# Local attention and a top-128 feed-forward on one core: 570 listed steps in place of nested loops

## The chip, the cores and the metric

The kernel runs on one core of a Trainium2 chip. The metric is device time in microseconds for one execution, median of several. The engines are PE (TensorE, with its weight loads shown as PEld), DVE (VectorE), ACT (ScalarE), POOL (GpSimd) and SP (SyncE, which here only issues DMAs). Each engine works through its own instructions in order; semaphores join them.

## The reference

q, k and v are 4 batches x 8 heads x 768 positions x 64 in float32. Attention is local: 24 chunks of 32 queries, each against 8 memory rows, 16 positions to the left, its own 32 and 8 to the right. The result x (4 x 768 x 512) goes through a gated feed-forward that touches only 128 rows of each batch:

```python
a = np.exp(scores - np.max(scores, axis=-1, keepdims=True))
out[:, :, c_start:c_end] = np.matmul(a / (a.sum(-1, keepdims=True) + 1e-09), v_full)
# then, for each batch b of x
scores = x @ w_gate
top_idx = np.argpartition(-scores[b], capacity)[:capacity]
h = np.maximum(x[b, top_idx] @ w1, 0.0)
ye = h @ w2
out[b, top_idx] = x[b, top_idx] + sigmoid(scores[b, top_idx])[:, None] * ye
```

w1 is 512 x 1024 and w2 is 1024 x 512.

## The kernel before, in words

Two heads make a pair, four pairs a batch: 16 pairs, n = 0 to 15. Each load brings 96 partitions of 8 positions for several heads, cast to 16 bit on the way, from POOL's DMA queue (`load`, L76); k, q and v come in groups of 2 or 4 heads, the memory rows and pads in four early DMAs and three from SP, the weights in two DMAs (`load_w`, L406).

A pair is worked in these parts. `t_k`, `t_q`, `t_v`: 16 PE transposes each into one PSUM bank (L161), an ACT copy out (L169, L172), and for k and v a small POOL copy that repeats the memory rows in every segment (L179, L185). `v_win`: 24 window transposes and 24 small products with the gate weights, alternating (L196, L197), then two DVE copies and one on ACT (L200, L202). `scores`: 48 products (L212) and a DVE maximum (L218). `soft`: four products that subtract the maximum (L226) and the exponential on ACT (L230). `t_p`: 12 transposes (L240) and a DVE copy, tile PT (L243). `values`: 48 products with 66 columns, of which column 64 is the sum of the probabilities and 65 the gate score (L260); DVE divides (L267 to L273), POOL casts the pair's columns of x to 16 bit for the gather (L275).

When a batch's four pairs are through, twelve expert steps go into a queue (`moe_steps`, L386): store x, spread the gate scores along rows, six compares on DVE (L318), counts on PE (L326), a scan over the mask (L334) and the slots, a one-hot selection, a gather by 24 products (L348), index and gate sums (L357), two halves of the first FFN product (L371), the second (L380), and a scatter that adds to the stored rows (L383). The main loop takes up to three of these steps in each round, between the parts of pairs n + 1 and n + 2; after the last pair the rest run one behind the other.

The order is that of the program text. Banks: one pair of banks for the scores, one for the values, four that turn for everything else.

Of the kernel before, what the change touches and what calls it, by code (L numbers as in the profile page):

```python
# [26 lines left out]
def kernel(  # L27
# [28 lines left out]
    VW = 66  # L56

    ctx.enter_context(tc.manual_schedule())

# [430 lines left out]
```

## Time and profile before

| | us |
|---|---|
| median of 3 runs (lowest, highest) | 192.08 (191.09, 194.02) |
| the profiled execution, its own time | 189.55 |
| its span in the trace | 187.8 |
| PE, DVE, ACT, POOL busy | 125.4, 92.9, 64.0, 55.0 |

The span runs from the first to the last instruction that the profiler recorded. Matmuls are pipelined, so their durations overlap; the distance between the starts of two groups is the better measure. Where an engine stood before an instruction, the trace names what ended the standing; "issue" means that nothing it shows did. DMA share is the mean busy share of 16 DMA engines and passes 1 where transfers overlap.

### The profile page before, as it was taken

To read this page: it belongs to the slowest core of one execution; us is meant where nothing else is said; L and a number is where in the kernel's file an instruction comes from. 1 tells how busy PE (TensorE), PEld (TensorE's weight loads), DVE (VectorE), ACT (ScalarE), POOL (GpSimd) and SP (SyncE) were. 2 spreads that over 40 slices of the span, in tenths; PEclk is the share of its full clock that TensorE was granted. 3 is DMA by queue.
4 is the path that set the end of the run, shared out by engine and by line. 5 is a ranking of instruction groups with operands and counts; after the bars stand their busy time and mean duration, and the time that the engine had idled before them with its cause. 6 is when DMAs were issued, how large, how long until landed. Compare 5 with 4: busy or idle time off the path is not lost. (4 is left out here: it accounts for less than half of the span.)

```text
span 187.8 us, 8103 instructions
## 1 busy us (share of the span) xinstructions
PE 125.4 (67%) x3780; PEld 106.1 (56%) x3780; DVE 92.9 (49%) x215; ACT 64.0 (34%) x105; POOL 55.0 (29%) x98
## 2 busy tenths in 40 slices
PE   0049847783938674598975496999769699435820
PEld 0048636672837573497764485886568588224800
DVE  0007434442533863626286877456598827565010
ACT  2025333332335240325635333463733344020300
POOL 7559260332860130203050302024222202310030
PEclk9999999999995555559999955999978579965795
DMA  5999999998799999500036200000670000075013
GB/s 55 96 153 193 207 205 207 198 123 146 105 153 246 286 219 206 89 0 7 5 48 244 106 7 0 7 3 3 130 270 3 3 3 3 7 174 213 0 7 49
DMA packets 15793, 19.65 MB, mean 105 GB/s; under 512 B 1293, under 2 KB 11629, under 8 KB 15757
## 3 DMA queue, kind: packets, MB, share of 16 engines
q0 software_dynamic: 11888, 12.75, 45.1%
q1 hardware_dynamic: 3872, 6.39, 10.7%
q8 instruction: 29, 0.48, 1.0%
q14 instruction: 4, 0.03, 0.1%
HBM read 23.40 MB, written 7.34 MB: 164 GB/s over the span
## 5 line engine op out<-in xcount | busy, mean ns | idle before, releaser
L196 PE MATMUL p_w<-ident,vT 128*64 128x128 f16 x384 | 27.9, 264 | 7.8 <-issue 7.8
L172 ACT COPY kT<-p_k 128x800 f16<-128x800 f16 x16 | 13.2, 826 | 53.6 <-PE p_k L161 53.6
L196 PEld LDWEIGHTS <-vT 128*64 128x64 f16 x384 | 25.8, 147 | 9.5 <-issue 8.2
L275 POOL CAST x<-x 128x768 f16<-128x768 f32 x16 | 14.4, 900 | 42.6 <-DVE x L270 42.0
L200 DVE COPY vw<-p_w 128x768 f16<-128x768 f16 x32 | 17.3, 554 | 19.1 <-PE p_w L196 9.6
L197 PE MATMUL p_w<-wgc,vT 128*64 128x2 f16 x384 | 26.3, 192 | 0.0
L197 PEld LDWEIGHTS <-vT 128*64 128x64 f16 x384 | 25.3, 139 | 1.3
L161 PE MATMUL p_k<-ident,kall 100*64 100x100 f16 x256 | 12.0, 252 | 15.1 <-DMA kall<-in_mem_k_dram 11.9
L185 POOL COPY vT<-vT 128x200 f16<-128x200 f16 x16 | 5.7, 354 | 54.9 <-ACT vT L172 54.9
L318 DVE TENSOR_SCALAR cmp<-brow,scr 128x768 f16<-128x768 f32 x24 | 15.3, 684 | 7.3 <-ACT brow L301 7.3
L260 PE MATMUL p_x<-vw,PT 64*32 64x66 f16 x768 | 9.8, 210 | 13.1 <-DVE PT L243 7.3
L161 PEld LDWEIGHTS <-kall 100*64 100x64 f16 x256 | 9.1, 139 | 16.1 <-issue 15.4
L270 DVE TENSOR_TENSOR x<-p_x,rd 128x384 f32<-128x384 f32 x32 | 16.4, 553 | 0.7
L260 PEld LDWEIGHTS <-PT 64*32 64x32 f16 x768 | 7.1, 95 | 15.6 <-DVE PT L243 9.6
L218 DVE TENSOR_REDUCE m<-p_s 128x12 bf16<-128x768 f32 x16 | 15.3, 955 | 0.8 <-PE p_s L212 0.8
L243 DVE COPY PT<-p_p 128x768 f16<-128x768 f16 x16 | 8.9, 555 | 12.3 <-PE p_p L240 12.3
L230 ACT ACTIVATE P<-p_s 128x768 f16<-128x768 f32 x16 | 13.0, 814 | 5.5 <-PE p_s L226 5.5
L202 ACT CAST vw<-p_w 128x24 f16<-128x24 f32 x16 | 4.3, 266 | 28.7 <-DVE vw L200 28.7
L172 ACT COPY vT<-p_v 128x800 f16<-128x800 f16 x16 | 13.3, 834 | 0.6 <-PE p_v L161 0.6
L169 ACT COPY qT<-p_q 128x768 f16<-128x768 f16 x16 | 13.0, 812 | 0.5 <-PE p_q L161 0.4
L383 POOL DMA_INDIRECT out_dram<-y,idx x4 | 6.4, 1610 | 22.2 <-DVE y L382 22.2
L161 PE MATMUL p_v<-ident,vall 100*64 100x100 f16 x256 | 11.9, 250 | 0.5 <-issue 0.5
(72 smaller groups left out, 214.8 us busy)
## 6 DMA issues: line engine op xcount, KB each, us to landing
out_dram<-x SPq DMA_DIRECT2D x8, 768.0 KB, 5.8
kall<-in_k_dram POOLq DMA_DIRECT2D x7, 384.0 KB, 10.0
qall<-in_q_dram POOLq DMA_DIRECT2D x7, 384.0 KB, 11.1
vall<-in_v_dram POOLq DMA_DIRECT2D x7, 384.0 KB, 12.4
w_sb<-in_moe_w_dram POOLq DMA_DIRECT2D x2, 1024.0 KB, 14.2
kall<-in_k_dram POOLq DMA_DIRECT2D x2, 192.0 KB, 7.5
qall<-in_q_dram POOLq DMA_DIRECT2D x2, 192.0 KB, 8.6
vall<-in_v_dram POOLq DMA_DIRECT2D x2, 192.0 KB, 8.1
```

What stands on the lines that cost most here:

```text
L161: nc.tensor.transpose(out=p[64 * h:64 * h + 64, rows * j:rows * j + rows], in_=src[:, 2 * n + h, 64 * j:64 * j + 64], identity=ident16[0:r ...
L169: nc.scalar.copy(out=qTs[n], in_=_sap(p, 0, [[1, 96], [96, 8]]))
L172: eng(out=t[:, :, 0:32].rearrange("p s (i j) -> p s i j", j=8), in_=_sap(p, 0, [[4, NSEG], [1, 4], [R, 8]]))
L196: nc.tensor.transpose(out=pw[i].bitcast(F16)[g, 128 * o:128 * o + 128], in_=win, identity=ident16)
L197: nc.tensor.matmul(out=pw[1][g, 384 + 2 * w:386 + 2 * w], lhsT=win, rhs=wgc[:, n % NP, :], start=True, stop=True, skip_group_check=True)
L200: nc.vector.tensor_copy(out=vw[:, 6 * i:6 * i + 6, :, 0:64], in_=pw[i].bitcast(F16)[:, 0:768].rearrange("p (w h d) -> p w h d", h=2, d=64))
L218: nc.vector.tensor_reduce(out=m, in_=s[:, :, 0:384].rearrange("p h (b k) -> p h b k", k=64), axis=AX.X, op=ALU.max)
L230: nc.scalar.activation(out=p, in_=s[:, :, 0:384].rearrange("p h (b k) -> p h b k", k=64), func=AF.Exp, scale=0.125)
L260: nc.tensor.matmul(out=X[32 * c:32 * c + 32, b2, VW * (2 * bp + h):VW * (2 * bp + h) + VW], lhsT=PT[o:o + 64, 3 * h + bp, 32 * c:32 * c + 32],
L270: nc.vector.tensor_tensor(out=x5[:, b2, :, 128 * pr:128 * pr + 128].rearrange("p g (h d) -> p g h d", d=D), in0=xv[:, b2, :, :, 0:64], in1 ...
L275: nc.gpsimd.tensor_copy(out=mods[b].x16[:, :, 128 * pr:128 * pr + 128], in_=xs[b][:, :, 128 * pr:128 * pr + 128])
L318: nc.vector.tensor_scalar(out=m.cmp[:, bl, :], in0=m.brow, scalar1=m.scr[:, bl:bl + 1], scalar2=None, op0=ALU.is_lt)
```

## The change

All parts become named steps, `NAME.number.engine`; one list, ORDER, holds them in the order in which they are issued, and a loop calls them. The letter gives the engine (p PE, v DVE, a ACT, g POOL, s SP); an eviction can be given to ACT or DVE, a compare to DVE or POOL. TK, TQ, TV are the transposes and EK, EQ, EV their evictions, FK and FV the POOL copies, Wa and Wb the windows with evictions Ea, Eb, VG, S the scores, R the maximum, A the shift, E the exponential, PT and EP the probabilities, PV the values, RC, GP and NM the division, ST the store; m marks expert steps: SC, B and R the rows, C the compares, T the counts, MK, IN, LT, SL, SE slots and selection, AU, IX, GS index and gate, GI, GT, G, X the gather, Fa, Fb, Ha, Hb, Ya, Yb, Y the FFN.

What differs beside the order: k, q and v live in five buffers of four heads each, with the pads loaded group by group; the pad row has moved, so the identity in the transposes of k and v is rotated. The window transposes of a half come first and the 24 gate products stand behind those of the second half. For batches 0 to 2 an indirect DMA fetches the 128 chosen rows from the stored output and four 32-bit transposes turn them; the 24 gathering products and the 16-bit cast stay for batch 3 alone, in four pieces. For batch 3 the sums and gate scores come from a product of their own (SG, 48 matmuls on columns 64 and 65), placed ahead of the products with the 64 value columns. One division instruction takes the place of two, four window buffers that of three.

```diff
+ORDER = """
+LK.0.g LQ.0.g C0.0.g CV.0.v LV.0.g CV.1.v CV.2.v CV.3.v CV.4.v C1.0.v LV.2.g LK.2.g LK.4.g LQ.2.g TK.0.p
+LV.4.g EK.0.a TQ.0.p FK.0.g EQ.0.v TV.0.p LQ.4.g EV.0.v LK.6.g S.0.p TK.1.p R.0.v TQ.1.p FV.0.g LV.6.g
+Wa.0.p EK.1.v EQ.1.a A.0.p Wb.0.p Ea.0.v E.0.a TV.1.p FK.1.g Eb.0.v LQ.6.g TK.2.p VG.0.a PT.0.p EV.1.a
+LK.8.g S.1.p EP.0.v EK.2.a TQ.2.p R.1.v PV.0.p FV.1.g EQ.2.a TV.2.p FK.2.g RC.0.v A.1.p LQ.8.g NM.0.v
+EV.2.a Wa.1.p Wb.1.p LV.8.g GP.0.v E.1.a Ea.1.v TK.3.p TQ.3.p Eb.1.v EK.3.a PT.1.p FV.2.g VG.1.v S.2.p
+LV.10.g EP.1.v EQ.3.a Wa.2.p R.2.v C2.0.g LW.0.g PV.1.p FK.3.g Wb.2.p RC.1.v LQ.10.g GP.1.v A.2.p NM.1.v
+TV.3.p LK.10.g E.2.a TQ.4.p Ea.2.v EV.3.a Eb.2.v PT.2.p LK.12.g S.3.p EP.2.v VG.2.a EQ.4.a TK.4.p R.3.v
+FV.3.g PV.2.p EK.4.a LV.12.g Wa.3.p RC.2.v A.3.p GP.2.v NM.2.v Wb.3.p E.3.a FK.4.g TV.4.p Ea.3.v LQ.12.g
+TK.5.p EV.4.a Eb.3.v S.4.p LK.14.g PT.3.p VG.3.a R.4.v EK.5.a TV.5.p TQ.5.p FV.4.g EP.3.v A.4.p EV.5.a
+FK.5.g Wa.4.p LQ.14.g PV.3.p EQ.5.a Ea.4.v Wb.4.p FV.5.g RC.3.v E.4.a LV.14.g GP.3.v TK.6.p NM.3.v TQ.6.p
...
+R.6.v PT.5.p mT0.0.p mT1.0.p mT2.0.p EP.5.v FK.7.g A.6.p mT3.0.p Ea.6.v mT4.0.p E.6.a PV.5.p Eb.6.v
+mT5.0.p VG.6.a RC.5.v PT.6.p NM.5.v S.7.p EP.6.a TV.7.p mMK.0.v GP.5.v TQ.8.p mIN.0.v EV.7.a R.7.v PV.6.p
+mLT.0.p TK.8.p EQ.8.a FV.7.g RC.6.v A.7.p NM.6.v Wa.7.p EK.8.a Wb.7.p mSL.0.v mSE.0.v E.7.a TV.8.p FK.8.g
+TK.9.p EV.8.a Ea.7.v S.8.p GP.6.v Eb.7.v VG.7.a mAU.0.p FV.8.g EK.9.a R.8.v PT.7.p Wa.8.p FK.9.g Wb.8.p
+mIX.0.v Ea.8.a mGS.0.v mGI.0.g EP.7.v A.8.p TQ.9.p VG.8.a Eb.8.v PV.7.p E.8.a TV.9.p RC.7.v EQ.9.a PT.8.p
...
+EQ.11.a R.10.v TK.11.p FV.10.g mGT.0.p EP.9.a mSC.1.v Wa.10.p mX0.0.v A.10.p EK.11.a mB0.1.p Ea.10.v
...
+RC.10.v NM.10.v mB1.1.p PT.11.p EV.12.a FK.12.g TQ.13.p GP.10.v S.12.p mR1.1.v EP.11.a FV.12.g mC4.1.v
+TK.14.p mC0.1.g Wa.12.p EQ.13.a mC5.1.v PV.11.p mC2.1.g Ea.12.v EK.14.a Wb.12.p RC.11.v NM.11.v TK.13.p
+mC3.1.g VG.12.a TV.13.p EK.13.a TQ.14.p Eb.12.v ST.2.s FK.14.g GP.11.v EV.13.a TV.14.p FK.13.g mSC.2.v
+R.12.v mB0.2.p mGX.2.a mB1.2.p FV.13.g EQ.14.a mC1.1.v A.12.p mR0.2.a mGD.2.v mT0.1.p mT1.1.p mT2.1.p
...
+SG.12.p E.13.a mAU.1.p Ea.14.v TK.15.p Eb.13.a RC.12.v S.14.p GP.12.v mGS.1.v PV.12.p mIX.1.v VG.13.a
+mC5.2.v mGI.1.g EK.15.a PT.13.p R.14.v Wb.14.p TV.15.p EP.13.v VG.14.a A.14.p FK.15.g Eb.14.a mT0.2.p
...
+Wb.15.p Ea.15.a mGS.2.v S.15.p mIX.2.v XC.13.a VG.15.v mGI.2.g SG.14.p R.15.v Eb.15.a mGT.1.p RC.14.v
+A.15.p mX0.1.a GP.14.v PV.14.p E.15.a mFa.1.p NM.14.v mFb.1.p XC.14.g mHa.1.v PT.15.p mHb.1.a mYa.1.p
+EP.15.v SG.15.p mYb.1.p RC.15.v GP.15.v mSC.3.v mGX.3.a mB0.3.p mGD.3.v mY.1.a mGT.2.p mSCAT.1.g PV.15.p
+mR0.3.a mX0.2.v mB1.3.p NM.15.v mFa.2.p mR1.3.a mC1.3.g mC4.3.v mFb.2.p XC.15.a ST.3.s mHa.2.v mC2.3.g
+mC0.3.v mYa.2.p mHb.2.a mC5.3.v mYb.2.p mC3.3.v mT0.3.p mT1.3.p mY.2.a mT2.3.p mT3.3.p mT4.3.p mT5.3.p
+mMK.3.v mIN.3.v mSCAT.2.g mLT.3.p mSL.3.v mSE.3.v mG0.3.p mG1.3.p mX0.3.a mG2.3.p mX1.3.a mAU.3.p mG3.3.p
+mX2.3.a mX3.3.v mIX.3.v mFa.3.p mGS.3.v mFb.3.p mHa.3.v mYa.3.p mHb.3.a mYb.3.p mY.3.a mSCAT.3.g
+"""
...
+    def LK(n, e):
+        first = n == 0
+        load(k, kls, 4, n, 0, 2 if first else 4)
+        nc.gpsimd.dma_start(out=kls[n // 2 % GB][0:4, :, :],
+                            in_=_dap(mem_k, 2 * n * 512, [[0, 4], [512, 4], [1, 512]]), max_dma_last_dim=512)
+    def LV(n, e):
+        first = n == 0
+        load(v, vls, 4, n, 0, 2 if first else 4)
+        nc.gpsimd.dma_start(out=vls[n // 2 % GB][1:2, :, :],
+                            in_=_dap(mem_v, 2 * n * 512, [[0, 1], [512, 4], [1, 512]]), max_dma_last_dim=512)
+        if first:
+            load(k, kls, 4, n, 2, 4)
+            load(q, qls, 0, n, 2, 4)
+            load(v, vls, 4, n, 2, 4)
...
+    def LW(n, e):
+        nc.gpsimd.dma_start(out=w1_sb, in_=_dap(moe_w1, 0, [[F, 128], [128 * F, 4], [1, F]]))
+        nc.gpsimd.dma_start(out=w2_sb, in_=_dap(moe_w2, 0, [[Dm, 128], [128 * Dm, 8], [1, Dm]]))
...
+        nc.vector.tensor_copy(out=rot16[:, 0:R - 1], in_=ident16[0:R, 1:R])
+        nc.vector.tensor_copy(out=rot16[:, R - 1:R], in_=ident16[0:R, 0:1])
...
+    def CV(n, e):
+        nc.vector.memset(vls[n][0:4, :, :], 0.0)
...
+    def FK(n, e):
+        mem_copy(pr_[n].kT)
...
+    def windows(n, i, p):
+        for o in range(6):
+            for half in range(2):
+                nc.tensor.transpose(out=p.bitcast(F16)[64 * half:64 * half + 64, 128 * o:128 * o + 128],
+                                    in_=win(n, 6 * i + o, half), identity=ident16)
+    def Wb(n, e):
+        p = pr_[n].pwb = bank32("p_wb")
+        windows(n, 1, p)
         for w in range(12):
             for half in range(2):
+                nc.tensor.matmul(out=p[64 * half:64 * half + 64, 384 + 2 * w:386 + 2 * w], lhsT=win(n, w, half),
+                                 rhs=wgc[:, n % NP, :], start=True, stop=True, skip_group_check=True)
...
+    def SG(n, e):
+        batch(n)
+        pr_[n].g = products(n, 64, 66)
+
+    def PV(n, e):
+        batch(n)
+        pr_[n].x = products(n, 0, 64 if n >= EARLY else 66)
+        if n < EARLY:
+            pr_[n].g = pr_[n].x[:, :, :, :, 64:66]
...
+    def RC(n, e):
+        s = pr_[n]
+        s.rd = sb4.tile([128, 2, 3, 2], FP, tag="rd", name="rd")
+        nc.vector.reciprocal(out=s.rd, in_=s.g[:, :, :, :, 0])
+
+    def NM(n, e):
+        s, b = pr_[n], n // NP
+        x5 = xs[b].rearrange("p (g b) m -> p b g m", b=2)[:, :, :, 128 * (n % NP):128 * (n % NP) + 128]
+        nc.vector.tensor_tensor(out=x5.rearrange("p b g (h d) -> p b g h d", d=D), in0=s.x[:, :, :, :, 0:64],
+                                in1=s.rd.unsqueeze(4).to_broadcast([128, 2, 3, 2, D]), op=ALU.mult)
...
+    outb = [_dap(out, 0, [[Dm, (b + 1) * S], [1, Dm]]) for b in range(B)]
...
+    def XC(n, e):
+        b = n // NP
+        if not hasattr(mods[b], "x16"):
+            mods[b].x16 = mod1.tile([128, NB, Dm], F16, tag="x16", name="x16")
+        o = 128 * (n % NP)
+        copy(e, mods[b].x16[:, :, o:o + 128], xs[b][:, :, o:o + 128])
...
+    def cmp_(b, bl, e):
+        m = mods[b]
+        if not hasattr(m, "cmp"):
+            m.cmp = [None] * NB
+        t = m.cmp[bl] = cst_cmp.tile([128, S], F16, tag="cmp", name="cmp")
+        (nc.vector if e == DVE else nc.gpsimd).tensor_scalar(out=t, in0=m.brow, scalar1=m.scr[:, bl:bl + 1],
+                                                             scalar2=None, op0=ALU.is_lt)
...
+    def mGI(b, e):
+        m = mods[b]
+        m.xg = mod1.tile([128, Dm], FP, tag="xg", name="xg")
+        nc.gpsimd.indirect_dma_start(out=m.xg[:, :], out_offset=None, in_=outb[b],
+                                     in_offset=bass.IndirectOffsetOnAxis(ap=m.idx[:, :1], axis=0))
+
+    def mGT(b, e):
+        m = mods[b]
+        m.pe = [bank32("p_e")]
+        for c in range(4):
+            nc.tensor.transpose(out=m.pe[0][:, 128 * c:128 * c + 128], in_=m.xg[:, 128 * c:128 * c + 128],
+                                identity=ident)
...
+    def gather(b, c):
+        m = mods[b]
+        if c == 0:
+            m.pe = []
+        m.pe.append(bank32("p_e"))
         for bl in range(NB):
...
+    def evict(b, c, e):
+        if len(mods[b].pe) == 1 and b < B - 1:
+            copy(e, xeT(b), mods[b].pe[0].rearrange("p (c t) -> p c t", t=128))
+        else:
+            copy(e, xeT(b)[:, c, :], mods[b].pe[c][:, 0:128])
...
+    def mSCAT(b, e):
+        m = mods[b]
+        nc.gpsimd.indirect_dma_start(out=outb[b], out_offset=bass.IndirectOffsetOnAxis(ap=m.idx[:, :1], axis=0),
+                                     in_=m.y[:, :], in_offset=None, compute_op=ALU.add)
+
...
+    for token in ORDER.split():
+        name, n, e = token.split(".")
+        steps[name](int(n), e)
```

## Rows read from the trace of the kernel before

**Rows 1.** The page's list of DMA queues: packets, megabytes, share of 16 engines.

```profile
q8 instruction: 29, 0.48, 1.0%
```

**Rows 2.** Busy time by stretch: stretch, length, each engine's busy time and instructions, clock, DMA, GB/s.

```profile
0.00:75.50 75.50, 44.51 (x1373) 38.86 (x1374) 30.50 (x71) 23.70 (x37) 32.17 (x65) 0.88 1.09 175
27.70:33.90 6.20, 3.96 (x128) 3.50 (x128) 2.07 (x3) 1.64 (x3) 0.39 (x2) 1.00 1.24 206
33.90:45.30 11.40, 7.91 (x256) 6.81 (x256) 5.20 (x12) 3.27 (x5) 4.24 (x7) 1.00 1.08 169
75.50:162.20 86.70, 70.65 (x2246) 59.27 (x2245) 54.49 (x122) 37.58 (x62) 19.09 (x31) 0.83 0.18 50
```

**Rows 3.** Timeline of PE, the groups behind its longest stops up to 76 us.

```profile
27.84 0.32 PE L196 MATMUL p_w<-ident,vT 128*64 128x128 f16 x2 [2.48 <-issue]
...
45.33 0.29 PE L161 MATMUL p_k<-ident,kall 100*64 100x100 f16 x2 [2.83 <-issue]
...
56.04 0.25 PE L196 MATMUL p_w<-ident,vT 128*64 128x128 f16 x2 [2.95 <-issue]
...
75.51 0.30 PE L260 MATMUL p_x<-vw,PT 64*32 64x66 f16 x13 [2.96 <-issue]
```

**Rows 4.** Waits of PE from 75.5 to 162.8 us: total us, times, longest.

```profile
PE p_x L260 <- DVE PT L243: 5.8, 9, 1.7
PE p_n L336 <- DVE incl L334: 4.9, 3, 1.8
```

**Rows 5.** Timeline of PE in a stretch at full clock: start, duration, line, tile, count.

```profile
119.15 0.53 PE L161 MATMUL p_q<-ident,qall 96*64 96x96 f16 x16
...
119.97 0.30 PE L357 MATMUL p_a<-aux,sel 128*128 128x3 f16 x6
120.20 0.53 PE L240 MATMUL p_p<-ident,P 128*64 128x128 f16 x12
...
122.34 1.07 PE L371 MATMUL p_h<-xeT,w_sb 128*128 128x128 f16 x16
123.34 0.52 PE L226 MATMUL p_s<-m,negi 128*64 128x384 bf16 x4
124.81 1.07 PE L371 MATMUL p_h<-xeT,w_sb 128*128 128x128 f16 x16
...
126.63 1.90 PE L380 MATMUL p_y<-w_sb,hT 128*128 128x512 f16 x8
128.46 0.53 PE L240 MATMUL p_p<-ident,P 128*64 128x128 f16 x12
```

**Rows 6.** Busy time in a stretch at half clock, columns as in rows 2.

```profile
63.70:68.38 4.68, 4.68 (x113) 4.27 (x101) 4.48 (x10) 2.10 (x4) 1.84 (x2) 0.50 1.18 257
```

**Rows 7.** Waits of POOL over the whole span: total us, times, longest.

```profile
POOL kall L77 <- DMA kall<-in_mem_k_dram: 2.4, 1, 2.4
...
POOL vall L77 <- DMA kall<-in_k_dram: 1.5, 1, 1.5
```

**Rows 8.** DMA issues: count, KB each, median us from issue to landing.

```profile
w_sb<-in_moe_w_dram POOLq DMA_DIRECT2D x2, 1024.0 KB, 14.2
```

**Rows 9.** Timeline of DVE and POOL: compares with and without a cast beside them.

```profile
139.71 1.71 DVE L318 TENSOR_SCALAR cmp<-brow,scr 128x768 f16<-128x768 f32 x2
...
142.27 1.13 DVE L318 TENSOR_SCALAR cmp<-brow,scr 128x768 f16<-128x768 f32 x2
...
147.00 0.83 POOL L275 CAST x<-x 128x768 f16<-128x768 f32 x1 [2.58 <-DVE x L270]
```

**Rows 10.** Timeline of the last stage.

```profile
162.21 0.56 PE L260 MATMUL p_x<-vw,PT 64*32 64x66 f16 x48 [0.85 <-DVE PT L243]
...
163.12 1.02 DVE L270 TENSOR_TENSOR x<-p_x,rd 128x384 f32<-128x384 f32 x2
...
172.48 2.74 PE L348 MATMUL p_e<-sel,x 128*128 128x128 f16 x24 [1.32 <-DVE sel L340]
...
180.81 1.56 POOL L383 DMA_INDIRECT out_dram<-y,idx  x1 [15.78 <-DVE y L382]
```

More of the change, by code (lines that the diff above doesn't have):

```diff
@@ L324, in m_count, with mAU @@
+    def mAU(b, e):
+        m = mods[b]
+        m.pa = bank32("p_a")
         for bl in range(NB):
-            for i in range(NB):
-                nc.tensor.matmul(out=m.pc[:, i:i + 1], lhsT=m.cmp[:, bl, 128 * i:128 * i + 128], rhs=ones1,
-                                 start=(bl == 0 and i == 0), stop=(bl == NB - 1), skip_group_check=True)
-    def m_slots(b):
+            nc.tensor.matmul(out=m.pa[:, 0:3], lhsT=m.sel[:, bl, :], rhs=auxs[b % 2][:, bl, :],
+                             start=(bl == 0), stop=(bl == NB - 1))
@@ L428 @@
-    t_v(1)
-    t_p(0)
-    for n in range(NPR):
-        m1 = scores(n + 1) if n + 1 < NPR else None
-        values(n)
-        if n % NP == NP - 1:
-            queue.extend(moe_steps(n // NP))
-        if n + 2 < NPR:
-            t_k(n + 2)
-        step()
-        if m1 is not None:
-            soft(n + 1, m1)
-            v_win(n + 1)
-        if n == 2:
-            load_w()
-        if later:
-            later.pop(0)()
-        step()
-        if n + 2 < NPR:
-            t_q(n + 2)
-            t_v(n + 2)
-        step()
-        if n + 1 < NPR:
-            t_p(n + 1)
@@ L453, with mFa, mFb, relu @@
-    while queue:
-        step()
+            for c in range(4):
+                nc.tensor.matmul(out=p[:, 128 * fi:128 * fi + 128], lhsT=w1_sb[:, c, f0:f0 + 128],
+                                 rhs=m.xeT[:, c, :], start=(c == 0), stop=(c == 3), skip_group_check=True)
+        return p
+    def mFa(b, e):
+        mods[b].pha = ffn1(b, 0)
+    def mFb(b, e):
+        mods[b].phb = ffn1(b, 1)
+    def relu(b, half, p, e):
+        m = mods[b]
+        if not hasattr(m, "hT"):
+            m.hT = mod2.tile([128, 8, 128], F16, tag="hT", name="hT")
+        o, i = m.hT[:, 4 * half:4 * half + 4, :], p.rearrange("p (c t) -> p c t", t=128)
+        if e == ACT:
+            nc.scalar.activation(out=o, in_=i, func=AF.Relu)
+        else:
+            nc.vector.tensor_scalar(out=o, in0=i, scalar1=0.0, scalar2=None, op0=ALU.max)
@@ new lines, in mHa, with mHb, mYa, mYb @@
+    def mHa(b, e):
+        relu(b, 0, mods[b].pha, e)
+    def mHb(b, e):
+        relu(b, 1, mods[b].phb, e)
+    def mYa(b, e):
+        m = mods[b]
+        m.py = bank32("p_y")
+        for f in range(4):
+            nc.tensor.matmul(out=m.py, lhsT=m.hT[:, f, :], rhs=w2_sb[:, f, :], start=(f == 0), stop=False)
+    def mYb(b, e):
+        m = mods[b]
+        for f in range(4, 8):
+            nc.tensor.matmul(out=m.py, lhsT=m.hT[:, f, :], rhs=w2_sb[:, f, :], start=False, stop=(f == 7))
+    def mY(b, e):
+        m = mods[b]
+        m.y = mod2.tile([128, Dm], FP, tag="y", name="y")
+        if e == ACT:
+            nc.scalar.mul(out=m.y, in_=m.py, mul=m.gate[:, 0:1])
+        else:
+            nc.vector.tensor_scalar(out=m.y, in0=m.py, scalar1=m.gate[:, 0:1], scalar2=None, op0=ALU.mult)
```

463 lines of the change are left out of this document (227 added, 236 removed).

## The prediction

> **What bounds the kernel now.** I read three views in this order: busy time by stretch, the PE timeline for what its stops end with, and the list of waits. The reader is to see three stages with three limits.
>
> Stage A, up to 75.5 us. DMA runs at a share above 1 throughout [rows 2], and PE stops again and again for 2.5 to 3 us with nothing named but "issue" [rows 3]. Between the stops stand whole multiples of 256 PE instructions: 128 + 128 in 6.20 us, 256 + 256 in 11.40 us [rows 2]. A queue of its own brings instructions in 29 packets of 16.5 KB [rows 1]; 29 times 256 is nearly all of the 7,560 PE instructions that the code issues (16 pairs of 416, 4 batches of 226). I read this as: PE's code comes in blocks of 256, and while q, k, v and weights fill the DMA engines each block takes about 6 us to come. PE gets 2,747 instructions by 75.5 us [rows 2], whatever their order.
>
> Stage B, to the last pair's value products at 162.2 us: 4,491 PE instructions in 86.70 us, PE busy 70.65, DVE 54.49, ACT 37.58, DMA share 0.18 [rows 2]. PE is the nearest bound. What is its work at full clock? In a dense stretch [rows 5] a pair costs q and v 0.82 (119.15 to 119.97), probability transposes, scores, values, k 2.14 (120.20 to 122.34), shift and windows 1.47 (123.34 to 124.81): 4.43 us for 416 instructions, 10.6 ns each. FFN halves cost 1.00 each (122.34 to 123.34), the second product 1.83 (126.63 to 128.46), index and gate sums 0.23 (119.97 to 120.20). Stage B holds 9.4 pairs (41.5), three batches of expert work at 4.06 (12.2), three gathers (5.6, an estimate: 1.9 each from the 2.74 that one took at half clock [rows 10]) and some 170 small instructions (1.8): 61 us. So 25.6 us are lost: 16.05 PE idle, the rest half clock (mean 0.83). Of the idle time 5.8 us wait for the eviction of the probabilities and 4.9 for the scan behind the counts [rows 4].
>
> Stage C, from the end of those products at 162.77 to 187.8 us: one chain of selection, gather, FFN and scatter, 25.0 us [rows 10].
>
> **The change, part by part.**
>
> *PE work.* Counted from the listing: 7,824 instructions (384 more for the last batch's separate gate products, 120 fewer in three gathers). By 75.5 us I give the new kernel the same 2,747, and 418 follow its last gate product, so 4,659 lie in stage B: 9.3 pairs (41.2), four gate products at 0.5, a quarter of the 2.14 above (2.0), FFN work of batch 0 and three quarters of batch 1 with index sums of three batches (7.4), some 225 small instructions (2.4): 53 us. Batch 2's FFN and gathering products are no longer in B. The windows' transposes and gate sums, interleaved before, now stand apart; the trace has no such sequence. Below, nothing changes; above, the gate sums stop hiding, 24 of them per pair at 10.6 ns for each of two instructions, 0.5 us, 5 us in all. I take 0, since the LDWEIGHTS and half alternation stay.
>
> *Waits in B.* The listing puts one to four other PE steps between each producer on DVE or ACT and its reader (PT.7, four steps, PV.7; mT5.0, five steps, mLT.0), which is what the 10.7 us of [rows 4] lack. In return PE meets new waits: banks, DVE order, and blocks of scores and values, 192 instructions in little over 1 us, faster than code has been seen to come. Loss in B: between 0 and today's 25.6. I take half, 13, for the two named waits and some clock return, 10.7 and about 2 of it, are what I can point at. B: 53 + 13 = 66, ending at 141.5.
>
> *Loads and stage A.* Loads move up the listing and k and v get a small pad DMA for each group: five DMAs for two pairs instead of three. POOL stood 1.5 us at its ninth DMA for the landing of the first, and 2.4 us at the tenth for the second [rows 7]: eight are in flight, and POOL stands in order. Behind the weights this bites. LV.12's pad is the 39th DMA and waits for w1, LQ.12 for w2, LK.14 for LQ.10 and LK.10; queued behind them on POOL are FK.4, FV.4 and FK.5, the copies that scores and windows of pairs 4 and 5 need. Five groups of q, k and v at 1.18 MB, LV.10 (0.39), weights (2.1), LQ.10 and LK.10 (0.79) are 9.2 MB by the code; at 206 GB/s [rows 2] 45 us from about 10, so FV.4 runs near 55 us, at PE instruction 1,864, where the fetch pace alone would have PE too (2,747 less 20.5 us at 6 us a block is 1,870). If the weights take 14.2 us each [rows 8], not the 5 that 206 GB/s gives, PE falls three blocks behind, though the later blocks then come faster. Price of stage A: 0 to +6; the first product may start 3 us earlier without the wide pads, but FK.0 stands behind the 17th DMA, so −3 to +6. I take 0, the fetch pace being the stricter row.
>
> The Trainium skill's "Runtime: NRT & Kernel Launch", Instruction fetch mechanics, has the same 256-instruction blocks but calls their cost "mostly hidden". The trace disagrees: 2.48 and 2.96 us stand open [rows 3]. By the page, stage A would be free to shrink; that is rival 1.
>
> *Gather.* Batches 0 to 2 fetch chosen rows from the stored output. ST, mGI and mGT stand far apart (mAU.1 to mGT.1: nine pair steps); the row for an indirect issue is 1.56 us [rows 10] and it and its landing hide. If mGI.2 comes late, mGT.2 holds the tail, by up to 6 us. POOL loses 12 casts of 0.83 [rows 9], already off the path: 0.
>
> *Compares on POOL.* 11 of 24. None is in the trace; nearest row, a POOL cast of equal size, 0.83 [rows 9]. In time it hides. But two DVE compares took 1.71 us while POOL cast, 1.13 when it didn't [rows 9]: 0.58 lost per meeting. Nine meetings in B are 5 us of DVE, which has slack; two in C, 1.2. Lower bound 0, upper rival 2.
>
> The Trainium skill's "SBUF — State Buffer", Who interferes with whom, says that the shared port is an exclusive lock and the loser stands for the whole instruction. By it a meeting costs 0.83, not 0.58, 3 us more over all eleven.
>
> *Tail.* The last batch's normalisation, 1.02 us [rows 10], leaves the chain; four compares instead of six on DVE save 1.1; the gather product runs in four pieces with eviction between, perhaps 1. Against this PE now does batch 2's FFN (3.8) and PV.15 in front of the counts, and DVE two evictions and NM.15 (some 2.2) between the compares. Net 0, between −2 and +3: 25.
>
> Sum: 75.5 + 66 + 25 = 166.5 of span. The profiled execution took 189.55 for a span of 187.8 and the runs' median is 192.08, so add 1.75 and 2.5: **171 us**.
>
> **Rivals.**
> 1. *Fetch stops are no law.* If the stops in A came of the old order's position and vanish, A loses the four stops of [rows 3], 11.2 us: 160. Against: multiples of 256, exactly.
> 2. *POOL becomes the bound.* If a compare costs three casts, 2.5 us, the eleven hold DVE or POOL for 27 us; with FK and FV copies queued behind them (mC2.1, mC3.1 ahead of FK.14) 15 to 22 of that show: 186 to 193, about no change. For: POOL meetings lengthen both sides. Against: a cast reads and writes the same sizes in 0.83.
> 3. *The clock stays at half.* k, shift, windows, q and v took 4.68 us at granted clock 0.50 [rows 6] against 2.76 at full (0.47 + 1.47 + 0.82 [rows 5]): 1.70 times. If the new order leaves PE stops of 2 to 3 us every 10 us, as the stop at 56.04 [rows 3], after which the clock reads 0.50 [rows 6], B becomes 53 × 1.70 = 90 plus 13, 37 more: 208; with half of B so, 190. Slower begins when over 0.7 of B runs at half clock. Against: fewer stops, so denser work.
> 4. *The early gate scores do nothing*, because SG.15 itself is late and DVE is behind: the tail then is 28, and the time 174. This lies in the forecast's range.
>
> **How the numbers follow.** About 2% is what a measurement tells: same is 188.2 to 195.9. Forecast 0.55, own range 159 to 185 (B's loss 3 to 22, A −3 to +6). Rival 1 0.12; rival 2 0.20, one in four of it still faster; rival 3 0.13, of it a tenth within 2%. Faster 0.55 + 0.12 + 0.04, about 0.71; same 0.16; slower 0.13. The range takes in rivals 1 and 2 and leaves out most of 3: 160 to 193.
>
> **What would show it.** A right: PE still at multiples of 256 with "issue" stops until the loads end, instruction 2,747 within 5 us of 75.5. B right: PE's waits for PT and for the scan under 3 us together, PE busy over 80% and clock above 0.85. POOL: FV.4 near 55 us, right behind the landing of w2. Compares: mean on POOL under 1.2 us. Tail: 23 to 28 us from SG.15's end. Wrong: a first row of waits in B above 8 us, whoever it names, a compare of 2.5 us, or stage A ending after 82.

## The result, and the profile after

The changed kernel took **181.08 us** (median of 4 runs, 180.12 to 184.81) against 191.67 beside it (191.09 to 194.02): ratio 0.943, 95% interval 0.937 to 0.950. It is faster, by 10.6 us, a little over half of the forecast gain; 171 was forecast, 10 us too low. Ratios, here and below, take only the runs within 1.5% of a kernel's fastest (with fewer than two of these none is given), medians take all runs, and the profiled execution is the longest of this kernel's runs, 184.81 us for a span of 183.1, so its stages are together some 4 us longer than the median's.

Busy time of the changed kernel by stage, columns as in [rows 2]:

```profile
0.00:77.30 77.30, 46.84 (x1404) 39.79 (x1404) 36.16 (x77) 23.21 (x35) 42.43 (x76) 1.00 1.03 174
77.30:156.00 78.70, 69.74 (x2305) 57.24 (x2303) 48.07 (x106) 40.29 (x60) 27.02 (x30) 0.70 0.18 57
156.00:183.10 27.10, 14.93 (x206) 11.60 (x205) 9.21 (x20) 5.93 (x12) 9.87 (x5) 0.80 0.36 88
```

Stage B lies in the middle row: 4,608 PE instructions in 78.7 us, 58.6 a microsecond, against 51.8 in [rows 2]. PE stands 9.0 us of it, 16.05 before. But the mean clock fell from 0.83 to 0.70: it was at 1.2 GHz from 80.2 to 93.8, 100.7 to 107.5 and 124.6 to 151.9 us.

The 1.00 of the first row is not what PE's own rows show. The same sixteen products last

```profile
62.63 0.85 PE L228 MATMUL p_q<-ident,ql 96*64 96x96 f16 x16
...
72.83 0.51 PE L228 MATMUL p_q<-ident,ql 96*64 96x96 f16 x16
```

so up to some 70 us PE worked at half clock here too. The clocks of [rows 2] for stage A (0.88 and 1.00) are too high in the same way: at 14.73 us of the kernel before these products took 0.85 us, against 0.53 in [rows 5]. In stage B the clock column agrees with the rows.

The page of the changed kernel, beside [rows 1] and [rows 9]:

```profile
q8 instruction: 30, 0.49, 1.1%
...
L469 POOL TENSOR_SCALAR cmp<-brow,scr 128x768 f16<-128x768 f32 x11 | 26.7, 2447 | 7.0 <-ACT brow L119 5.9
```

A compare on POOL takes 2.45 us, three casts. PE's waits in stage B of the changed kernel (77.3 to 155.5 us), beside [rows 4]:

```profile
PE p_s L312 <- issue: 5.4, 3, 3.1
PE p_k L228 <- issue: 1.4, 1, 1.4
PE p_x L372 <- issue: 1.3, 3, 0.6
PE p_c L477 <- POOL cmp L469: 0.6, 1, 0.6
```

The waits for the probabilities and the scan, 10.7 us before, are gone; what is left is nearly all "issue". PE's timeline of the changed kernel, beside [rows 3]:

```profile
29.62 0.32 PE L228 MATMUL p_v<-rot,vl 100*64 100x100 f16 x3 [2.23 <-issue]
...
42.11 0.54 PE L228 MATMUL p_v<-rot,vl 100*64 100x100 f16 x7 [2.15 <-issue]
...
48.51 0.35 PE L372 MATMUL p_x<-vw,PT 64*32 64x66 f16 x20 [2.89 <-issue]
...
101.53 0.60 PE L312 MATMUL p_s<-kT,qT 64*32 64x64 f16 x46 [3.07 <-issue]
...
122.85 0.54 PE L228 MATMUL p_k<-rot,kl 100*64 100x100 f16 x15 [1.41 <-issue]
129.45 0.41 PE L312 MATMUL p_s<-kT,qT 64*32 64x64 f16 x30 [1.58 <-issue]
```

Counted over all matmuls, weight loads and semaphore instructions of PE, these stops stand before PE instructions 705, 1,217, 1,473, 4,289, 5,569 and 5,825, each 193 past a multiple of 256: stage B has the stops at block ends too. The kernel before had one such stop there, of 2.4 us, also before instruction 4,289; the prediction gave these stops no term in stage B:

```profile
107.33 0.25 PE L196 MATMUL p_w<-ident,vT 128*64 128x128 f16 x2 [2.40 <-issue]
```

POOL of the changed kernel, beside [rows 7]:

```profile
50.98 0.69 POOL L131 DMA_DIRECT2D ql<-in_q_dram  x1 [4.21 <-DMA w_sb<-in_moe_w_dram]
...
55.45 0.36 POOL L250 COPY vT<-vT 128x200 f16<-128x200 f16 x1
```

FV.4 runs at 55.45, behind a stand of 4.21 us for w2. The tail of the changed kernel, beside [rows 10]:

```profile
154.66 0.50 PE L372 MATMUL p_x<-vw,PT 64*32 64x2 f16 x48
...
158.72 5.11 POOL L469 TENSOR_SCALAR cmp<-brow,scr 128x768 f16<-128x768 f32 x2
158.87 1.28 DVE L469 TENSOR_SCALAR cmp<-brow,scr 128x768 f16<-128x768 f32 x1
...
160.67 2.49 DVE L469 TENSOR_SCALAR cmp<-brow,scr 128x768 f16<-128x768 f32 x3
...
163.89 0.75 PE L477 MATMUL p_c<-ones,cmp 128*128 128x1 f16 x24 [0.91 <-POOL cmp L469]
...
169.29 3.52 PE L565 MATMUL p_h<-xeT,w_sb 128*128 128x128 f16 x32
...
175.65 1.57 POOL L612 DMA_INDIRECT out_dram<-y,idx  x1 [10.05 <-ACT y L606]
```

DVE is through with its four compares at 163.2, but the counts wait for POOL's two until 163.89. From SG.15's end (155.2) to the end are 27.9 us, against 25.0.

### The profile page after: what moved, and what is told of

The parts are those of the page before. It is cut to its first block, busy times and chain, and to the rows that moved or that the text cites. A ratio compares the mean times of both kernels' runs of the same rounds, so it can differ in the third digit from the quotient of the medians.

```text
span 183.1 us, 8400 instructions
## 1 busy us (share of the span) xinstructions
PE 131.5 (72%) x3912; PEld 108.6 (59%) x3912; DVE 93.4 (51%) x201; ACT 69.4 (38%) x107; POOL 79.3 (43%) x110
## 4 chain that ended last, share of the span: by engine, by line
PE 52%; issue 21%; POOL 11%; DMA 10%; DVE 3%; POOLq 1%
DMA out_dram<-y,idx 5%; POOL cmp L469 5%; PE p_x L372 5%; PE p_v L228 5%; PE p_p L346 5%; PE p_wa L273 5%; PE p_s L330 5%; DMA kl<-in_k_dram 4%; PE p_k L228 4%; PE p_wb L273 4%; PE p_s L312 4%; PE p_wb L285 4%; PE p_q L228 4%; PE p_b L430 2%; PE p_c L477 2%
## 5 line engine op out<-in xcount | busy, mean ns | idle before, releaser
L469 POOL TENSOR_SCALAR cmp<-brow,scr 128x768 f16<-128x768 f32 x11 | 26.7, 2447 | 7.0 <-ACT brow L119 5.9
L312 PE MATMUL p_s<-kT,qT 64*32 64x64 f16 x768 | 10.4, 221 | 16.5 <-issue 9.5
L273 PEld LDWEIGHTS <-vT 128*64 128x64 f16 x384 | 18.6, 151 | 4.4 <-POOL vT L250 1.4
L250 POOL COPY vT<-vT 128x200 f16<-128x200 f16 x16 | 6.1, 380 | 29.3 <-ACT vT L119 21.5
L228 PE MATMUL p_k<-rot,kl 100*64 100x100 f16 x256 | 12.7, 262 | 8.4 <-DMA kl<-in_mem_k_dram 5.7
L372 PE MATMUL p_x<-vw,PT 64*32 64x66 f16 (+2 forms) x960 | 12.7, 212 | 5.9 <-issue 5.9
L228 PE MATMUL p_v<-rot,vl 100*64 100x100 f16 x256 | 12.8, 261 | 5.7 <-issue 4.4
L402 DVE TENSOR_TENSOR x<-p_x,rd 128x768 f32<-128x768 f32 x16 | 15.3, 954 | 2.3 <-PE p_x L372 1.9
L273 PE MATMUL p_wa<-ident,vT 128*64 128x128 f16 x192 | 12.0, 285 | 1.1 <-POOL vT L250 1.1
L330 PE MATMUL p_s<-m,negi 128*64 128x384 bf16 x64 | 12.4, 485 | 0.0
L346 PE MATMUL p_p<-ident,P 128*64 128x128 f16 x192 | 12.0, 285 | 0.4 <-issue 0.4
```

Source lines behind the costliest of these rows:

```text
L228: nc.tensor.transpose(out=p[64 * h:64 * h + 64, rows * j:rows * j + rows], in_=src[n // 2 % GB][0:rows, 2 * (n % 2) + h, 64 * j:64 * j + 6 ...
L273: nc.tensor.transpose(out=p.bitcast(F16)[64 * half:64 * half + 64, 128 * o:128 * o + 128], in_=win(n, 6 * i + o, half), identity=ident16)
L312: nc.tensor.matmul(out=s.s[32 * c:32 * c + 32, h, 64 * blk:64 * blk + 64], lhsT=qf[64 * h:64 * h + 64, 32 * ch:32 * ch + 32], rhs=kf[64 * ...
L330: nc.tensor.matmul(out=s.s[g, h, 0:384], lhsT=negi[:, g], rhs=s.m[:, h, :].unsqueeze(2).to_broadcast([128, NB, 64]), start=False, stop=Tru ...
L346: nc.tensor.transpose(out=p[64 * b2:64 * b2 + 64, 128 * i:128 * i + 128], in_=s.P[:, h, 2 * bp + b2, :], identity=ident16)
L372: nc.tensor.matmul(out=X[32 * c:32 * c + 32, b2, w * (2 * bp + h):w * (2 * bp + h) + w], lhsT=s.PT[o:o + 64, 3 * h + bp, 32 * c:32 * c + 3 ...
```

## The experiments

My theory after the result: stage B lacks clock (some 12 us, what it measured above the forecast 66), the tail lacks the time of POOL's compares (2 to 3 us), stage A is tied to the loads. The rivals are in the expectations.

The table holds all twelve. Stage B is taken here from the first score product of pair 7 to the first score row of the last batch, from each kernel's profiled execution; the instructions are matmuls and weight loads. The tail is what follows. The row of the changed kernel is of its longest execution. With the median's span (some 179.4 us), the same start and the same tail its stage B would be some 73 us, 61 instructions a microsecond; this is an estimate, and it holds if the excess lies in stage B.

| kernel | median us | ratio to before (95%) | stage B us | of it at 1.2 GHz | PE instructions per us | tail us |
|---|---|---|---|---|---|---|
| changed | 181.08 | 0.943 (0.937–0.950) | 76.6 | 47.8 | 58.1 | 26.9 |
| e1_cmp_dve | 178.24 | 0.933 (0.925–0.940) | 74.2 | 43.9 | 60.0 | 24.8 |
| e2_fk_early | 179.61 | 0.945 (0.935–0.955) | 72.2 | 23.9 | 61.6 | 27.0 |
| e3_few_loads | 165.85 | 0.869 (0.860–0.878) | 72.6 | 21.2 | 61.3 | 24.6 |
| e4_dummy | 186.86 | none | 79.4 | 32.4 | 56.6 | 26.1 |
| e5_scores_together | 181.30 | 0.947 (0.939–0.956) | 69.6 | 27.3 | 59.8 | 28.0 |
| e6_gather_products | 183.56 | 0.957 (0.949–0.964) | 74.4 | 23.9 | 60.9 | 26.4 |
| e7_short_bursts | 183.31 | 0.956 (0.947–0.965) | 75.6 | 17.1 | 59.3 | 25.8 |
| e8_dve_batch1_early | 180.48 | 0.940 (0.931–0.949) | 72.9 | 21.7 | 61.0 | 25.8 |
| e9_split_stores | 180.03 | 0.944 (0.932–0.956) | 72.3 | 32.0 | 61.6 | 25.9 |
| e10_merged | 179.50 | 0.944 (0.935–0.953) | 73.6 | 33.3 | 58.5 | 25.8 |
| e11_all | 175.07 | 0.902 (0.889–0.915) | 74.4 | 27.3 | 57.9 | 24.9 |
| e12_all_together | 170.85 | none (before: 192.51) | 66.0 | 20.2 | 60.9 | 24.5 |

**e1_cmp_dve**: all compares on DVE.

```diff
-mC5.0.g mC4.0.g mC3.0.g mC0.1.g mC2.1.g mC3.1.g mC2.2.g mC1.2.g mC0.2.g mC1.3.g mC2.3.g
+the same eleven steps with .v
```

> All 11 compares of POOL go to DVE, nothing else changes. The changed kernel ran in about 181 us, and its POOL compares took 2.45 us each in the trace. Theory (they hold the path: in the last stage the counts wait for them, and FV.6 and FK.7 stand behind three of them): 176 to 179, POOL busy 27 us less, last stage 1 to 2 us shorter. Rival (they are off the path, and DVE gets 11 more compares of 0.57 us): 181 to 184.

178.24 us. The tail of this kernel, DVE alone:

```profile
151.51 0.50 PE L365 MATMUL p_x<-vw,PT 64*32 64x2 f16 x48
...
155.65 1.14 DVE L462 TENSOR_SCALAR cmp<-brow,scr 128x768 f16<-128x768 f32 x2
...
157.30 2.20 DVE L462 TENSOR_SCALAR cmp<-brow,scr 128x768 f16<-128x768 f32 x4
158.97 1.17 PEld L470 LDWEIGHTS <-cmp 128*128 128x128 f16 x36
```

Six compares take 3.34 us, and PE no longer stands before the last 24 counts. The eleven on POOL cost the change 2.8 us by the medians, 2.1 of it in the tail (26.9 to 24.8), and no run of this kernel (up to 179.45) is as long as the shortest of the changed one (180.12). Met.

**e2_fk_early**: the first 30 steps in another order, FK.0 and FV.0 ahead of the loads that stood before them.

```diff
-... TK.0.p LV.4.g EK.0.a TQ.0.p FK.0.g EQ.0.v TV.0.p LQ.4.g ...
+... C1.0.v TK.0.p EK.0.a FK.0.g LV.2.g LK.2.g TQ.0.p EQ.0.v TV.0.p ...
```

> Only the first 30 steps change places: FK.0 and FV.0 come before the loads that made POOL stand, so the first scores can start near 11 us, not 17.6. Theory (the pace of stage A is one block of 256 PE instructions per 6 us, counted from its first request): all of stage A moves ahead by 4 to 5 us, total 176 to 178. Rival (stage A ends with the loads, whenever PE began): 180 to 182, with longer stops in between.

179.61 us. PE instruction 2,753 came at 74.7 instead of 75.9 us. The first score product waited 7.0 us for FK.0 in the changed kernel and started at 17.27 us; here it waits for another copy, EQ.0 on DVE, and starts at 14.41, and the score product of the next pair waits for its own copy, FK.1. PE's waits up to 77.3 us of this kernel:

```profile
PE p_s L305 <- DVE qT L114: 4.8, 1, 4.8
...
PE p_s L305 <- POOL kT L243: 2.6, 1, 2.6
```

The rival is nearer, 179.61 lying between both ranges: the wait moved, and stage A came to its end 1.2 us earlier, not 4 to 5.

**e3_few_loads**: the loads of heads 8 to 31 are left out; their pairs compute with the data of the first eight heads.

```diff
 def LK(n, e):
+    if n > 2:
+        return
```

(the same in LQ and LV, and the tile index taken modulo 2).

> Left out: the loads of q, k and v for heads 8 to 31; their pairs work on the data of heads 0 to 7. Weights and stores stay. Theory (the block fetch is slow because loads fill the DMA engines): PE's stops at multiples of 256 instructions are gone after some 30 us, PE instruction 2,753 falls at 60 to 66 us in place of 77, total 166 to 171. Rival (the order or the evictions hold stage A): stops remain, total 179 to 182.

165.85 us, just below the theory's range. The stretch up to instruction 2,753 in this kernel:

```profile
0.00:62.90 62.90, 38.00 (x1378) 33.07 (x1380) 35.40 (x75) 23.18 (x35) 23.61 (x47) 0.85 0.56 99
```

Instruction 2,753 came at 62.6 us instead of 75.9, at a DMA share of 0.56 instead of 1.03. The code's packets on q8 come 4.5 us apart between 26 and 66 us (6.1 in the changed kernel). The stops are not all gone after 30 us, as the theory had it: two big ones are left, 4.0 and 2.8 us at 31 and 38 us, while the weights load. Stage A is indeed code that waits behind loads.

**e4_dummy**: two bursts of twelve full-array 128x512 products, whose result is not used, after mLT.0 and mB1.2.

```diff
+def ZZ(n, e):
+    p = bank32("p_z")
+    for i in range(12):
+        nc.tensor.matmul(out=p, lhsT=w1_sb[:, i % 4, 0:128], rhs=w1_sb[:, i % 4, 128:640],
+                         start=(i == 0), stop=(i == 11))
```

> Adds two bursts of 12 full-array products (128 x 128 weights, 512 columns), one behind mLT.0 (near 82 us), one behind mB1.2 (near 125 us), whose result nobody reads. They cost 2.6 us each at full clock, 5.1 at half. Theory (in stage B the clock fell to half because the pair work alone does not keep it up, while gathering products and FFN do): the granted clock is 1.00 for most of the 10 us behind each burst, the pair work there is 1.57 times as fast, total 174 to 180. Rival (the clock goes its own way, or follows stops alone): no rise behind the bursts, total 186 to 191.

186.86 us, slower than the change. The clock did follow. From the end of the first burst on, e4_dummy, then the changed kernel in the same stretch:

```profile
86.69:94.00 7.31, 6.88 (x315) 6.33 (x316) 3.85 (x11) 5.87 (x10) 2.17 (x4) 1.00 0.09 16
```

```profile
86.69:94.00 7.31, 7.31 (x232) 6.64 (x230) 3.42 (x9) 4.74 (x8) 1.82 (x3) 0.51 0.16 41
```

At nearly twice the clock PE did 315 products in place of 232, 1.36 times as many. So the theory's mechanism is there. But the bursts take 3.9 and 2.7 us themselves (82.78 to 86.69, 126.33 to 129.01), 6.6 together, and the kernel is 5.8 us longer than the changed one: all that the clock gave back is about 1 us, by the medians. That asked for a test with cheaper bursts.

**e7_short_bursts**: six bursts of three such products, after mLT.0, mAU.0, mB1.2, mLT.1, S.14 and SG.13.

> The changed kernel with six bursts of three full-array 128x512 products (no use made of them) in the stretches where the clock stood at 1.2 GHz. Theory (stage B's missing time is the clock, and full-array work brings it up): 1.2 GHz for under 25 of stage B's 78 us, total 172 to 179 us, though the bursts themselves take 4 to 8 us of TensorE. Rival (TensorE's clock is not what stage B lacks, or three products are too few): 184 to 190 us, 1.2 GHz for 40 us or more.

183.31 us. The clause on the clock was met, 17.1 us at 1.2 GHz instead of 47.8; the time came out just below the rival's range. The stretch up to the start of SG.15 in e7_short_bursts, then the same work, without the bursts, in the changed kernel:

```profile
77.00:153.45 76.45, 63.16 (x2273) 50.10 (x2269) 48.36 (x103) 40.10 (x60) 27.14 (x30) 0.89 0.19 59
```

```profile
77.30:154.65 77.35, 68.39 (x2253) 56.52 (x2251) 47.46 (x103) 40.29 (x60) 27.02 (x30) 0.69 0.18 58
```

PE's busy time falls by 5.2 us, bursts included, the stretch by 0.9. The six bursts take 4.7 us of it, from the start of each to that of the next instruction, so the pairs' own work became some 5.6 us shorter and the bursts took most of that. At 1.70 [rows 5, 6] the 30 us fewer at half clock would have been worth 12. Much of the rest went into standing: PE works faster and stands 13.3 us instead of 9.0. Where it stands, from PE's timeline of e7_short_bursts:

```profile
83.33 0.32 PE L221 MATMUL p_k<-rot,kl 100*64 100x100 f16 x5 [1.00 <-issue]
...
87.30 0.23 PE L305 MATMUL p_s<-kT,qT 64*32 64x64 f16 x10 [1.16 <-issue]
...
100.40 0.31 PE L221 MATMUL p_q<-ident,ql 96*64 96x96 f16 x4 [2.96 <-issue]
```

These are block ends again (instructions 3,265, 3,521 and 4,289). The starts of q8's packets in this trace (us):

```
73.30  76.81  80.59  84.47  88.34  92.07  98.03  101.51  106.14  109.60
```

One follows the other by 3.5 to 3.9 us where no store is under way, and each starts about 1.1 us after the stop before it has ended (83.33, then 84.47). At full clock PE works off 256 instructions sooner than that (83.33 to 85.94) and stands. In none of the fourteen traces do two packets behind 16 us start less than 3.2 us apart. From mLT.0 to the gather of the first batch both kernels need 21.5 us (81.1 to 102.6 and 82.0 to 103.5), one at full clock up to 100.5 and with two bursts in it (1.5 us), the other at half clock until 93.8.

**e8_dve_batch1_early**: e1_cmp_dve, the second batch's selection 17 to 28 steps earlier, the use of its gathered rows and its FFN 43 to 50.

> All compares on VectorE as in e1_cmp_dve, and the second batch's selection moved some 28 steps earlier, its gather and MLP some 52 steps earlier (its full-array products then stand within the stretch of 1.2 GHz, and out of the tail's neighbourhood). Theory (the clock is what stage B lacks): the 1.2 GHz stretch of 123 to 150 us is cut by 8 us or more, total 172 to 176 us. Rival (the order of the selection is indifferent, TensorE has the same work): 177 to 180 us as e1_cmp_dve.

180.48 us; half clock fell from 43.9 us to 21.7, the time didn't. The rival is nearer (its range ends at 180). This is the cleanest pair: as many instructions in stage B, no bursts, and all compares on DVE in both. Stage B of e1_cmp_dve, then of e8_dve_batch1_early:

```profile
78.75:152.93 74.18, 67.86 (x2228) 55.92 (x2226) 47.95 (x109) 39.43 (x59) 12.10 (x22) 0.70 0.19 61
```

```profile
78.61:151.55 72.94, 59.47 (x2228) 49.03 (x2226) 48.18 (x109) 39.71 (x60) 13.74 (x23) 0.85 0.22 65
```

At 1.70 the 22 us would be worth 9; the stage is 1.2 us shorter, and PE stands 13.5 us of it instead of 6.3.

**e9_split_stores**: the stores of batches 1 and 2 in six transfers each.

```diff
-ST.1.s ... ST.2.s
+SU.6.s (nine steps) SU.7.s (nine steps) ... SU.17.s
```

> The changed kernel with the stores of the second and third batch cut into six transfers each, nine steps apart. Theory (TensorE's code comes block after block, one transfer at a time, 3.4 us or more apart, and two big stores delay a block by 1.5 to 3 us each): the stops at instructions 4,289 and 5,569 to 5,825 shrink below 1.5 us, total 176 to 180 us. Rival (the stores' effect is small beside the clock's): 180 to 182 us.

180.03 us, on the edge between both ranges. The stops that were named shrank as the theory had it, to 0.2 us at instruction 4,289, 1.1 at 5,569 and none at 5,825. But others stand in their place: 1.6 us at the block end 4,033, and inside a block, at 6,015,

```profile
128.68 0.53 PE L267 MATMUL p_wa<-ident,vT 128*64 128x128 f16 x12 [2.69 <-POOL vT L244]
```

PE waits for FV, which stands behind two compares on POOL (122.93 to 128.34). The same windows wait 1.1 to 2.7 us for it in e2_fk_early, e4_dummy, e6_gather_products, e7_short_bursts and e10_merged, all at full clock, and not in the changed kernel, whose PE was at half clock there. On the time the run is inconclusive.

**e5_scores_together**: the last batch's gate scores come out of the value products again.

```diff
-EARLY = NPR - NP
+EARLY = NPR
-SG.n.p ... PV.n.p      (n = 12 to 15)
+PV.n.p in SG.n's place
```

> The changed kernel, but the last batch's gate scores come out of the value products again: no separate two-column products, the 66-column products stand at their place in the order. Theory (early gate scores bring little, and their 192 products cost 1.2 to 2.2 us of a half-clock TensorE per pair): total 176 to 180 us, stage B 3 to 5 us shorter, the tail at most 1 us longer. Rival (the separate gate scores start the last selection earlier by as much as they cost): 181 to 184 us, tail 2 us or more longer.

181.30 us, neither side's in full: stage B came out at 69.6 us, 7.0 less (some 3 less than the estimate for the changed kernel's median), and the tail at 28.0, the longest. In the tail of this kernel POOL and DVE meet once more:

```profile
151.55 5.60 POOL L462 TENSOR_SCALAR cmp<-brow,scr 128x768 f16<-128x768 f32 x2
152.00 2.76 DVE L462 TENSOR_SCALAR cmp<-brow,scr 128x768 f16<-128x768 f32 x1
```

One DVE compare takes 2.76 us there. So the gain could have been lost to the compares; e12_all_together takes that up.

**e6_gather_products**: the first three batches gather by 24 products from a 16-bit copy of x again, with 12 casts on POOL and no indirect load.

> The changed kernel with the gather of the first three batches undone: 24 full-array products per batch against a float16 copy of x, in place of an indirect transfer and four transposes; POOL makes the copies (12 casts). Theory (the gather by transfer is hidden and saves the products' TensorE time): 182 to 186 us, 1 to 2 us more TensorE per batch, POOL 10 us busier. Rival (the full-array products hold the clock at 2.4 GHz for longer, which is worth more than they cost): 177 to 180 us, fewer than 40 of stage B's 78 us at 1.2 GHz (48 in the changed kernel).

183.56 us: the gather by transfer is worth some 2.5 us (the two intervals just touch). Its products are full-array work, and half clock fell to 23.9 us; here too that didn't pay.

**e10_merged**: transposes of P two blocks at a time, the shift for all partitions at once; the same result with 8 products fewer for a pair.

```diff
-for b2 in range(2):
-    nc.tensor.transpose(out=p[64 * b2:64 * b2 + 64, ...], in_=s.P[:, h, 2 * bp + b2, :], ...)
+nc.tensor.transpose(out=p[:, ...], in_=s.P[:, h, 2 * bp:2 * bp + 2, :], ...)
-for g in (slice(0, 64), slice(64, 128)): ... lhsT=negi[:, g]
+lhsT=negi
```

> The changed kernel with 8 products fewer for each of the 16 pairs and the same result: the twelve 128x64 transposes of P become six 128x128 ones, the four products of the subtracted maxima two. Theory (code blocks are a limit of stages A and B alike: 256 instructions are saved, one block of 3.5 to 6 us, and the six are full-array work that brings the clock up): 174 to 178 us. Rival (instructions are not what limits): 180 to 182 us.

179.50 us: 1.6 less by the medians, where a block fewer should have given 3.5 to 6; by the ratios (0.944 and 0.943) there is no difference. The rival is nearer. A group of transposes at full clock in e10_merged:

```profile
87.00 0.49 PE L337 MATMUL p_p<-ident,P 128*128 128x128 f16 x6
```

Six 128x128 transposes last about as long as twelve 128x64 ones (0.53 in [rows 5]). The count of instructions is thus not the whole limit either: e10_merged and e11_all, which do the same work in fewer instructions, have low rates (58.5 and 57.9).

**e11_all**: e1_cmp_dve, e2_fk_early and e10_merged in one.

> The merged products of e10_merged, all compares on VectorE (e1_cmp_dve) and the first steps in the order of e2_fk_early. Theory: the gains add up as far as they lie in different stages (tail 2.5 us, code block 4 us, start 1 us): 171 to 176 us. Rival (each gives back what the other gained): 177 to 179 us, as e1_cmp_dve.

175.07 us, ratio 0.902. The three single gains of the medians (2.8, 1.5, 1.6 us) add up to 5.9; 6.0 were measured, inside the theory's range. By the ratios it looks otherwise: e2_fk_early (0.945) and e10_merged (0.944) are no faster than the changed kernel (0.943), e1_cmp_dve takes 1.0% off, and the three together 4.1%. So it is shown that the three together help, and not that they add up. A possible reason, not tested: e10_merged alone waited 4.2 us in stage B for FV and for compares on POOL, which e11_all doesn't.

**e12_all_together**: e11_all and e5_scores_together.

> e11_all with the last batch's gate scores out of the value products again, as in e5_scores_together, where stage B came out some 4 us shorter and the tail longer by as much, with slow compares on POOL in it. Theory (without those compares the tail no longer gives the gain back, and 384 instructions less count): 169 to 173 us. Rival (the early scores start the last selection as much earlier as they cost): 174 to 177 us, as e11_all.

170.85 us (165.20 to 172.84) against 192.51 beside it, 0.887 of it, and faster than both kernels. The tail stays (24.9 and 24.5 us), stage B goes from 74.4 to 66.0. With the compares out of the way the separate gate products cost about 4 us, by the medians of two sets of runs (175.07 and 170.85); the sets overlap (171.22 to 177.84 and 165.20 to 172.84). Stage B of e12_all_together:

```profile
77.00:141.50 64.50, 57.70 (x1957) 47.37 (x1952) 46.25 (x104) 38.54 (x57) 12.84 (x22) 0.85 0.22 69
```

3,909 instructions in 64.5 us, 60.6 a microsecond: the rate of the others, with less to do.

## Why the prediction was right, and where it was short

*Stage A*: right. Instruction 2,753 at 75.9 us (75.5 and 2,747 forecast), FV.4 at 55.45 (55), stops at multiples of 256; e3_few_loads shows that the loads make them long. Rival 1 is out. I would not have expected code stops to cost as much in stage B.

The sentence of the Trainium skill's "Runtime: NRT & Kernel Launch", Instruction fetch mechanics, that the cost of a block is "mostly hidden", does not fit stage A, where from instruction 705 on PE stops at nearly every block end. It fits stage B of the changed kernel in part: 11 of the 18 block ends there pass without a stop, and the other seven cost 8.1 us together, the three "issue" rows of PE's waits.

*Waits in B*: right. PT and the scan, 10.7 us in [rows 4], are off the list, PE is 89% busy. That the whole gain is 10.6 us between the medians is chance: by the sums work left stage B as well (61 to 53 us), half clock came into it, and the tail grew by 2.9 us. No run puts the two waits back, so their share of the gain is read from the traces alone.

*Loss in B*: the step that failed. Of the 25.6 us that were lost before I took off the two named waits and about 2 us of clock and kept 13: some 5 us of standing and 7.5 of half clock. The work was sized well: 47.7 of the 78.7 us were at half clock, which at 1.70 [rows 5, 6] are 28 at full; with the other 22 busy that is 50 us of work against 53 (the half-clock stretches taken as busy throughout). The loss was 29 us in this execution, 9 of standing and 20 of clock, and some 25 by the estimate for the median. Of the standing 8.1 us are stops at block ends, for which the sum had no term. Denser work didn't bring the clock: between 84 and 94 us PE was busy without a break and at 0.51:

```profile
84.00:94.00 10.00, 10.00 (x300) 9.33 (x298) 5.09 (x13) 5.68 (x10) 2.29 (x4) 0.51 0.12 32
```

"Clock above 0.85" was wrong (0.70).

And the clock is not the cause that could be mended alone. Five kernels had 17 to 24 us at 1.2 GHz and no fewer instructions in B (e2, e3, e6, e7, e8): their rates are 59.3 to 61.6 instructions a microsecond, 60.8 in the mean; e9, with 32.0 us, has 61.6, and e1, with 43.9, 60.0. The 1% between e1 and the five is some 1 us of the stage. The 58.1 of the changed kernel is of its longest execution, and the estimate for its median is 61. Right behind the clock stand the next limits: the code's blocks, 3.2 us apart at the least, with stops at their ends, and FV behind the compares on POOL. I priced loss as a sum of terms, where the terms take each other's place. What sets the 60 in full stays open: e10_merged saves a block and gained 1.6 us, less than half of what one takes, and e12_all_together shortened B by 8.4 us where its 288 fewer instructions at 60 make 4.8.

Two slips in the working change nothing: at rival 3's own 1.70 the gathers of the kernel before are 1.6 us each at full clock, not 1.9, so its work in B was 60 us, not 61; and one in four of rival 2's 0.20 is 0.05, not 0.04.

*Compares on POOL*: the nearest row (0.83) was wrong, rival 2's price (2.5) right: 2.45. Its consequence was not: 2.8 us by e1_cmp_dve, not 15 to 22. POOL had the room (27.0 us busy of 78.7 in B), and FK and FV had slack as long as PE was slow; in six kernels with more clock PE did wait for FV behind them, up to 2.7 us (e9_split_stores), so rival 2's path is there and was mis-sized. DVE's own compares lasted 0.62 us in the mean in e1_cmp_dve and 0.84 to 0.98 in the nine kernels where POOL had its share.

By the Trainium skill's "SBUF — State Buffer", Who interferes with whom, the loser of the port stands for the whole instruction, 2.45 us. The traces agree for one meeting only. In the changed kernel two DVE compares beside POOL's three took 1.80 us together:

```profile
118.06 1.80 DVE L469 TENSOR_SCALAR cmp<-brow,scr 128x768 f16<-128x768 f32 x2
118.12 6.99 POOL L469 TENSOR_SCALAR cmp<-brow,scr 128x768 f16<-128x768 f32 x3
```

Of the 114 DVE compares that overlapped one of POOL's in those nine kernels, 113 took 0.61 to 1.32 us; the 2.76 us in e5_scores_together is the one that comes near it. POOL pays too: its compares took 2.19 to 2.20 us where none of DVE's overlapped, and up to 3.41 where one did.

*Tail*: 27.9, the upper end of my range (25, −2 to +3), for the reason in e1_cmp_dve: counts behind POOL's compares.

*Gather*: hidden, as said, and worth 2.5 us (e6_gather_products). *Windows apart*: nothing to see; at half clock windows, gate sums and shift took 83.08 to 85.66 in the changed kernel, 2.58 us, which is 1.75 times the 1.47 of [rows 5].

*Rival 4*, early gate scores that do nothing: true, and more. They cost about 4 us by the medians once nothing else hides it (e11_all to e12_all_together). *Rival 3*, half clock: it happened for 48 of the 78.7 us, more than the half for which the rival had 190, and cost far less than 1.70 times, since PE at full clock stands instead (e7_short_bursts, e8_dve_batch1_early). The time stayed inside my range, 159 to 185, because of that and not because the clock was foreseen.

## What to carry to other kernels

Before pricing a slow clock or a wait, ask what PE would meet next if it went away, and look for it in a stretch where it already is away. Count the instructions of a stage and divide by its time: where the quotient stays nearly the same over several variants, take work out rather than reorder it. Price an operation on an engine that has never done it by a run of it; a cast of the same size was wrong by three.
